# Retention attention on array quarters in 64-token steps, Strassen from the second block, and a new order of the first loads: what the change did to a kernel bound by TensorE

## The chip, the cores and the metric

The kernel runs on one core of one Trainium2 chip. The metric is device time in microseconds (us); a run is one execution on the chip, and a time quoted as "median" is the median of the runs of one kernel in one session. "Span" is the time from the first to the last instruction in the profile of one execution. The profile also gives the granted clock of TensorE, 1.000 being full speed.

Engine names: PE is TensorE (PEld its weight loads), DVE is VectorE, ACT is ScalarE, POOL is GpSimd, SP is SyncE, which here only issues DMA.

## The reference

Retention attention (8 batches, 8 heads, 576 tokens, head size 64) feeds a feed-forward layer with the activation h·cos(h):

```python
scores = q @ k.T / sqrt(64)                          # per batch and head
ret    = scores * where(i >= j, gamma[h] ** (i - j), 0)   # gamma[h] = 1 - 2**(-5-h)
x      = (ret @ v) -> [4608 tokens, 512]
h      = x @ w_in                                    # [4608, 2048], the "first product"
out    = (h * cos(h)) @ w_out                        # [4608, 512],  the "second product"
```

## The kernel before

Attention runs chunk by chunk. The decay is folded into q and v, so one chunk needs four groups of matmuls: *inter* (queries against the state that earlier chunks left), *state* (add k·v of this chunk), *intra* (masked scores against v), and *scores* of the next chunk. The tokens go through the feed-forward layer in nine blocks of 512. The second product uses one level of Strassen (7 half-size products in place of 8) from block 2 on.

A chunk here is 128 tokens of one batch, five per batch (the fifth has 64). State, intra and scores use half of the 128x128 array per matmul, and matmuls on the two halves overlap (in the trace of this kernel, from 204.74 us, those of intra start in pairs 3 ns apart, a pair of 128 columns every 56 to 59 ns):

```python
def mm_intra(self, g, box):
    ...
    for c in range(4):
        for hp in range(2):                       # two halves of the array
            inst = e.matmul(
                ap(self.BK[box.i], 512, 64 * hp, 64, c * 128, [1, n]),      # n = 128 tokens
                ap(na, 2 * DM, 0, n, DM + (2 * c + hp) * D, [1, D]),
                ap(pt, 1024, 0, n, hp * 512 + c * 128, [1, n]), ...)
```

Nothing is issued in program order. The program is a list of operations with what each reads and writes. A scheduler that runs when the kernel is built (`arrange`) plays them through with estimated costs and a simple model of the DMA rings. It fixes the order of instructions on every engine, hands out PSUM banks, and puts *filler* matmuls (on zeros) where it believes PE idle in the first 24 us. On the chip every engine then works through its fixed list and waits on semaphores: an operation placed early in the list holds up everything behind it.

The start-up:

```python
load_to(4)                                        # q, k, v of the first four chunks, on SP's queue
for g in range(4):
    self.cast_k(g, "act")
    if pair(g):
        self.cast_q(dbl(g), ("dve", "pool"))      # the two halves of the q weighting
    self.cast_v(g, "dve" if g == 3 else "pool")
    self.step_tk(g, "act")                        # transposes of k on PE, copied out by ACT
    if pair(g):
        self.step_tq(dbl(g), "dve")
    self.step_s(g); self.step_st(g); self.step_o(g)   # state and output copies on ACT
self.load_win(0, 1, [("stg", 1, 1)])              # w_in, on POOL's queue: not before v of chunk 1
self.load_win(1, 1, [("stg", 1, 1)])
self.load_win(2, 2, [("stg", 2, 1)])              # not before v of chunk 2
self.load_win(4, 2, [("stg", 2, 1)])
self.load_win(6, 2, [("stg", 2, 1)])
for x in range(4):
    self.load_wout(x, [("stg", 2, 1)])
load_to(9, [("wout", 2)])                         # block 1's q, k, v: only after w_out
... # then mlp1 (first product) of block 0
```

Block 0 is the first 512 tokens: four chunks. Their attention has to be done before "dense" work, the unbroken row of first-product matmuls, can begin. "Gates" below are the third arguments of `load_win`: what a load waits for before it is issued.

Of the kernel before, what the change touches and what calls it, by code (L numbers as in the profile page):

```python
# [14 lines left out]
CH = 128  # L15
CHUNKS = [(b, r, min(CH, S - CH * r)) for b in range(B) for r in range(5)]
TB = 512
NTB = TOK // TB
FILL, SLOW = 24.0, 5.6
NF = DFF // 128  # L20
HF, HB = NF // 2, TB // 2
XR = 3 * TB

# [9 lines left out]
class Op:  # L33
    __slots__ = ("eng", "fn", "r", "w", "sem", "cost", "ring", "deps", "need", "val", "snap",
                 "n", "out", "n_in", "start", "boxes", "seq", "port", "lazy")
# [6 lines left out]
class Prog:  # L42

    LAT = {"pe": 0.2, "act": 0.11, "dve": 0.14, "pool": 0.14, "sp": 0.0}
    WINDOW = {"pe": 24, "act": 12, "dve": 12, "pool": 6, "sp": 4}
# [8 lines left out]
    def add(self, eng, fn, r=(), w=(), sem=None, cost=0.1, ring=None, port=False, lazy=False):  # L54
        op = Op(eng, fn, list(r), list(w), sem, cost, ring)
        op.port, op.lazy = port, lazy
        self.ops.append(op)
        return op


    def arrange(self, filler, fill_until):
# [40 lines left out]
        while left:  # L102
            for eng in queue:
                while free[eng] <= now:
                    pick = None
                    for op in queue[eng][:self.WINDOW[eng]]:
                        if op not in ready or ready[op] > now:
                            continue
                        if any(b.i is None for b in op.boxes) and not banks:
                            continue  # L110
                        if op.ring and eng == "sp" and len(rings["sp"]) >= 4:
                            continue
                        if pick is None or not op.lazy:
                            pick = op
                        if not pick.lazy:
                            break
                    if pick is None:
                        if eng == "pe" and 1.4 <= now < fill_until:
                            op = Op("pe", filler, ["one", "dum"], ["fill"], None, 0.108, None)
# [3 lines left out]
                        break  # L123
                    for b in pick.boxes:
                        if b.i is None:
                            b.i = banks.pop(0)
# [23 lines left out]
            for h in heads:  # L150
                h[1] -= step / len(heads)
            for q in rings.values():
                if q and q[0][1] <= 0:
                    done.append((now + 1.25, q.pop(0)[0]))
# [65 lines left out]

def ap(t, size, p0, n, off, *dims):
# [3 lines left out]
class Kernel:  # L225
    def __init__(self, nc, es, q, k, v, w_in, w_out, out):
        self.nc = nc
        self.P = Prog(nc, es, 5)
# [3 lines left out]
        self.NSTG, self.NNAT, self.NKT, self.NQ, self.NQT = 5, 6, 5, 3, 4  # L232
# [11 lines left out]
        self.SBD = [sb(f"sbd{i}", [128, 512], BF16) for i in range(self.NSB)]  # L244
# [7 lines left out]
        self.WT = sb("wt", [128, 88], F32)  # L252
        self.IDN = sb("idn", [128, 128], BF16)
        self.TRI = sb("tri", [128, 128], BF16)
        self.ONE = sb("one", [128, 128], BF16)
        self.DUM = sb("dum", [128, 512], BF16)
        self.IV = sb("iv", [128, 88], F32)
        self.LV = sb("lv", [128, 88], F32)
        self.CLN = sb("cln", [128, 1], F32)
        self.CPI = sb("cpi", [128, 1], F32)  # L260
        self.SC = nc.alloc_psum_tensor("sc", [128, 1024], F32)
        self.ST = nc.alloc_psum_tensor("st", [128, 512], F32)
        self.BK = [nc.alloc_psum_tensor(f"bk{i}", [128, 512], F32) for i in range(5)]
        self.n_cb = self.n_os = 0

# [10 lines left out]
    def constants(self):  # L276
        P = self.P
        lng = [math.log(1.0 - 2.0 ** (-5.0 - h)) for h in range(H)]
        P.add("pool", lambda e: e.iota(ap(self.IV, 88, 0, 128, 0, [1, 40]), [[128, 5], [0, 8]], base=0,
                                       channel_multiplier=1, allow_small_or_imprecise_dtypes=True), w=["iv0"])  # L280
        P.add("pool", lambda e: e.iota(ap(self.IV, 88, 0, 128, 40, [1, 48]), [[256, 3], [1, 2], [0, 8]], base=0,
                                       channel_multiplier=2, allow_small_or_imprecise_dtypes=True), w=["iv1"])
        P.add("dve", lambda e: e.memset(self.ONE.ap(), 1.0), w=["one"])
        P.add("dve", lambda e: e.memset(self.DUM.ap(), 0.0), w=["dum"])
        for h in range(H):
            P.add("dve", lambda e, h=h: e.memset(ap(self.LV, 88, 0, 128, h, [8, 5]), -lng[h]), w=[("lv", h)], cost=0.03)
            P.add("dve", lambda e, h=h: e.memset(ap(self.LV, 88, 0, 128, 40 + h, [8, 6]), lng[h]), w=[("lv", h + 8)], cost=0.03)
        P.add("dve", lambda e: e.memset(self.CLN.ap(), math.log(1.0 / 8.0)), w=["cln"])
        P.add("dve", lambda e: e.memset(self.CPI.ap(), math.pi / 2), w=["cpi"])
        P.add("dve", lambda e: e.tensor_tensor(self.LV.ap(), self.IV.ap(), self.LV.ap(), ALU.mult),  # L290
              r=["iv0", "iv1"] + [("lv", h) for h in range(16)], w=["lvx"])
        for i in range(self.NSB):
            P.add("dve", lambda e, i=i: e.memset(self.SBD[i].ap(), 0.0), w=[("sbd", i)])
        P.add("act", lambda e: e.activation(ap(self.WT, 88, 0, 128, 0, [1, 40]), ap(self.LV, 88, 0, 128, 0, [1, 40]),
                                            AF.Exp), r=["lvx"], w=["wv"], cost=0.25)
        P.add("act", lambda e: e.activation(ap(self.WT, 88, 0, 128, 40, [1, 48]), ap(self.LV, 88, 0, 128, 40, [1, 48]),
                                            AF.Exp, bias=self.CLN.ap()), r=["lvx", "cln"], w=["wq"], cost=0.3)
# [3 lines left out]
        P.add("pool", lambda e: e.affine_select(self.TRI.ap(), self.ONE.ap(), pattern=[[1, 2], [2, 64]],  # L301
                                                compare_op=ALU.is_ge, fill=0.0, base=0,
                                                channel_multiplier=-1), r=["one"], w=["tri"])
# [7 lines left out]
    def load_kv(self, g, i, gate=()):  # L311
        b, r, n = CHUNKS[g]
        slot = g % self.NSTG
        self.P.add("sp", lambda e: e.dma_start(  # L314
            ap(self.STG[slot], 2 * DM, 0, n, i * DM, [D, H], [1, D]),
            bass.AP(self.src[1 + i], (b * H * S + CH * r) * D, [[D, n], [S * D, H], [1, D]])),
            r=list(gate), w=[("stg", slot, i)], sem=f"i{slot}_{i}", cost=0.6, ring=1.24 * n / 128)

    def load_q(self, d, gate=()):
        b, r = d // 3, d % 3  # L320
        n, slot = (128, 128, 32)[r], d % self.NQ
        self.P.add("sp", lambda e: e.dma_start(  # L322
            ap(self.QSTG[slot], 2 * DM, 0, n, 0, [2 * D, H], [1, 2 * D]),
            bass.AP(self.src[0], (b * H * S + 256 * r) * D, [[2 * D, n], [S * D, H], [1, 2 * D]])),
            r=list(gate), w=[("qstg", slot)], sem=f"q{slot}", cost=0.6, ring=1.81 * n / 128)

    def load_win(self, s, n, gate=()):
# [3 lines left out]
            r=list(gate), w=[("win", x) for x in range(s, s + n)], sem=f"wi{s}", cost=0.78, ring=1.3 * n)  # L331

    def load_wout(self, s, gate=()):
# [3 lines left out]
            r=list(gate), w=[("wout", s)], sem=f"wo{s}", cost=0.78, ring=2.6)  # L337
# [9 lines left out]
    def cast_k(self, g, eng):  # L347
        n, st, na = CHUNKS[g][2], g % self.NSTG, g % self.NNAT
        self.copy(eng, ap(self.NAT[na], 2 * DM, 0, n, 0, [1, DM]), ap(self.STG[st], 2 * DM, 0, n, 0, [1, DM]),
                  [("stg", st, 0)], [("nat", na, 0)], DM)  # L350

    def cast_v(self, g, eng):
        b, r, n = CHUNKS[g]
        st, na = g % self.NSTG, g % self.NNAT
        self.P.add(eng, lambda e: e.tensor_tensor(  # L355
            ap(self.NAT[na], 2 * DM, 0, n, DM, [D, H], [1, D]),
            ap(self.STG[st], 2 * DM, 0, n, DM, [D, H], [1, D]),
            ap(self.WT, 88, 0, n, 8 * r, [1, H], [0, D]), ALU.mult),
            r=[("stg", st, 1), "wv"], w=[("nat", na, 1)], cost=1.04 if eng == "pool" else 0.62, port=True)

    def cast_q(self, d, engs):
        n, k = (128, 128, 32)[d % 3], d % self.NQ
        for x, eng in enumerate(engs):
            self.P.add(eng, lambda e, x=x: e.tensor_tensor(  # L364
                ap(self.QNAT[k], 2 * DM, 0, n, x * DM, [D, H], [1, D]),
                ap(self.QSTG[k], 2 * DM, 0, n, x * D, [2 * D, H], [1, D]),
                ap(self.WT, 88, 0, n, 40 + 16 * (d % 3) + 8 * x, [1, H], [0, D]), ALU.mult),
                r=[("qstg", k), "wq"], w=[("qnat", k, x)], cost=1.04 if eng == "pool" else 0.62, port=True)

    def step_tk(self, g, eng="act"):  # L370
        n, k, box = CHUNKS[g][2], g % self.NNAT, Box()

        def mm(e):
            tb = self.BK[box.i].ap().bitcast(BF16)
            for c in range(4):
                inst = e.transpose(
                    tb[:, c * 128:c * 128 + n], ap(self.NAT[k], 2 * DM, 0, n, 128 * c, [1, 128]),
                    ap(self.IDN, 128, 0, n, 0, [1, n]))
            return inst

        self.P.add("pe", mm, r=[("nat", k, 0), "idn"], w=[box], cost=0.22)
        t = g % self.NKT
        dst = ap(self.KT[t], DM, 0, 128, 0, [128, 4], [1, n])

        def src():
            return self.BK[box.i].ap().bitcast(BF16)[:, 0:512].rearrange("p (c n) -> p c n", c=4)[:, :, 0:n]

        if eng == "act":
            self.P.add("act", lambda e: e.activation(dst, src(), AF.Copy), r=[box], w=[("kt", t)], cost=0.56)
        else:  # L390
            self.P.add("dve", lambda e: e.tensor_copy(dst, src()), r=[box], w=[("kt", t)], cost=0.36)

    def step_tq(self, d, eng="act"):
# [567 lines left out]
```

## Time and profile before

| | before |
|---|---|
| time, median of 3 runs | 306.48 us (306.26 to 306.99) |
| span, granted clock | 305.5 us, 1.000 |
| PE busy | 294.2 us, 96% |
| DVE / ACT / POOL busy | 76% / 58% / 51% |

The two rows below come from the page's part in which the span is cut in 40 slices, each digit a busy share in tenths; PEclk is the granted clock. The page of the kernel before:

```profile
PE   8999998999999999999999999999999999999996
...
PEclk9999999999999999999999999999999999999999
```

PE is busy everywhere, at full clock. A change pays only if it takes work or waiting from PE.

The timeline of PE of the kernel before, one attention step in mid-run (start us, us, engine, line, operation, out<-in, array tile, size, count; bracketed: idle before):

```profile
204.27 0.39 PE L473 MATMUL bk<-qt,sbd 128*128 128x128 bf16 x4
204.59 0.32 PE L458 MATMUL st<-nat 128*64 128x64 bf16 x8
204.74 0.39 PE L487 MATMUL bk<-pt,nat 128*64 128x128 bf16 x8
205.06 0.40 PE L443 MATMUL sc<-qt,kt 64*128 64x128 bf16 x8
205.39 0.28 PE L694 MATMUL bk<-wout,gt 128*128 128x256 bf16 x1
```

Read start to start, for ends are modelled: 204.27 to 205.39 is 1.12 us for 128 tokens, in inter 0.32, state 0.15, intra 0.32 and scores 0.33. Where the array tile changes (inter to state, intra to scores, scores to the dense matmul) the next start comes 149 to 152 ns after the last, where within inter, intra and scores it comes 52 to 62 ns after; this excess of about 0.1 us is the "mode change" of the prediction.

The last line of start-up on PE is the beginning of the dense work:

```profile
23.61 3.61 PE L575 MATMUL bk<-xt,win 128*128 128x256 bf16 x31
```

The chain of waits of the kernel before (start us, us, what), where the loads of block 1 come in:

```profile
19.34 16.31 DMA wout<-in_moe_w_out_dram
...
38.48 6.45 DMA qstg<-in_q_dram
...
47.10 0.62 PE bk L401 x8
```

w_out holds back a load of q, and PE's transposes (L401) wait for that q. It is the longest (1.4 us) of several pauses between 35 and 60 us, 3.2 us in all.

### The profile page before, as it was taken

What the parts mean: (1) busy time and instruction counts of PE and PEld (TensorE: products, weight loads), DVE (VectorE), ACT (ScalarE), POOL (GpSimd) and SP (SyncE); (2) the same over time, 40 slices, a digit from 0 to 9 for tenths busy, and PEclk for the clock granted to TensorE, in tenths of its full rate; (3) what the DMA queues carried; (4) which work ended last, traced back from release to release, by engine and by line L of the source; (5) the groups of instructions that cost most, each with busy time, mean ns of one, the idle gap of its engine ahead of it and who ended that gap; (6) DMA issues with size and microseconds to landing.
All of it is one profiled execution on the core that took longest, in us unless ns stands there. A gap on an engine that the chain in (4) does not pass through costs nothing.

```text
span 305.5 us, 7008 instructions
## 1 busy us (share of the span) xinstructions
PE 294.2 (96%) x2756; PEld 195.3 (64%) x2792; DVE 233.6 (76%) x349; ACT 176.1 (58%) x306; POOL 155.5 (51%) x159
## 2 busy tenths in 40 slices
PE   8999998999999999999999999999999999999996
PEld 6667434678554446766676577666765766666585
DVE  2566623789968999779899996996899669948941
ACT  5667511698466686366656656475656566546411
POOL 2870068968576664788369754854450014003213
PEclk9999999999999999999999999999999999999999
DMA  8999999999999999999999999796202100211114
GB/s 182 231 196 195 190 207 248 241 255 198 221 202 198 199 227 213 175 255 199 219 211 206 220 169 243 186 223 138 55 17 72 36 24 12 70 36 34 34 36 137
DMA packets 134432, 48.95 MB, mean 160 GB/s; under 512 B 103168, under 2 KB 133376, under 8 KB 134400
## 3 DMA queue, kind: packets, MB, share of 16 engines
q1 hardware_dynamic: 129648, 44.32, 69.3%
q0 software_dynamic: 4752, 4.19, 8.7%
q8 instruction: 22, 0.36, 0.5%
q14 instruction: 10, 0.08, 0.1%
HBM read 36.70 MB, written 9.44 MB: 151 GB/s over the span
## 4 chain that ended last, share of the span: by engine, by line
PE 75%; DMA 9%; DVE 5%; SPq 3%; issue 2%; POOL 2%; ACT 1%; DVEq 0%
PE bk L575 33%; PE bk L694 25%; PE bk L600 6%; DMA wout<-in_moe_w_out_dram 5%; PE sc L443 3%; SPq L314 3%; PE bk L487 2%; DVE gt L586 2%; DMA qstg<-in_q_dram 2%; PE st L458 2%; DMA stg<-in_v_dram 2%; PE bk L473 2%; DVE s L656 1%; SPq L322 1%; POOL win L328 1%
## 5 line engine op out<-in xcount | busy, mean ns | idle before, releaser
L575 PE MATMUL bk<-xt,win 128*128 128x512 bf16 (+3 forms) x642 | 133.3, 347 | 3.4 <-issue 0.8
L583 ACT ACTIVATE cb<-bk,cpi 128x512 bf16<-128x512 f32 (+2 forms) x152 | 100.1, 665 | 57.2 <-PE bk L575 55.0
L586 DVE TENSOR_TENSOR gt<-bk,cb 128x512 bf16<-128x512 f32 (+2 forms) x152 | 97.5, 657 | 33.8 <-ACT cb L583 32.4
L575 PEld LDWEIGHTS bk<-xt,win 128*128 128x128 bf16 x672 | 62.6, 98 | 47.3 <-ACT xt L530 1.7
L364 POOL TENSOR_TENSOR qnat<-qstg,wt 128x512 bf16<-128x512 f32 (+1 forms) x46 | 51.4, 1133 | 18.6 <-DMA qstg<-in_q_dram 18.5
L345 POOL CAST nat<-stg 128x512 bf16<-128x512 f32 (+1 forms) x36 | 24.3, 676 | 52.2 <-DMA stg<-in_k_dram 35.3
L511 DVE TENSOR_TENSOR pt<-sc,tri 128x1024 bf16<-128x1024 f32 (+1 forms) x40 | 44.3, 1107 | 8.6 <-PE sc L443 8.6
L720 POOL TENSOR_TENSOR sv<-sv,os 128x512 f32<-128x512 f32 x14 | 21.0, 1499 | 54.4 <-DVE gt L586 27.7
L355 POOL TENSOR_TENSOR nat<-stg,wt 128x512 bf16<-128x512 f32 (+1 forms) x39 | 43.6, 1117 | 2.1 <-DMA stg<-in_v_dram 1.7
L530 ACT ACTIVATE xt<-bk 128x512 bf16<-128x512 f32 (+1 forms) x41 | 27.7, 679 | 21.2 <-PE sc L443 19.8
L600 PE MATMUL bk<-wout,gt 128*128 128x512 bf16 x122 | 29.6, 379 | 0.3
L663 DVE TENSOR_TENSOR gt<-gt 128x1024 bf16<-128x1024 bf16 x28 | 28.9, 1034 | 0.0
L694 PE MATMUL bk<-tw,gt 128*128 128x256 bf16 x224 | 28.6, 273 | 0.0
L694 PE MATMUL bk<-wout,gt 128*128 128x256 bf16 x224 | 27.6, 273 | 0.9 <-DVE gt L586 0.9
L694 PE MATMUL bk<-wout,s 128*128 128x256 bf16 x224 | 27.1, 273 | 0.0
L694 PEld LDWEIGHTS bk<-wout,gt 128*128 128x128 bf16 x224 | 21.4, 98 | 7.3 <-DVE gt L586 1.8
L694 PEld LDWEIGHTS bk<-tw,gt 128*128 128x128 bf16 x224 | 21.3, 98 | 7.5 <-ACT sv L724 1.3
L656 DVE TENSOR_TENSOR s<-gt 128x1024 bf16<-128x1024 bf16 x28 | 23.5, 857 | 2.2 <-PE bk L694 2.2
L694 PEld LDWEIGHTS bk<-wout,s 128*128 128x128 bf16 x224 | 21.6, 98 | 4.9
L342 ACT ACTIVATE sbd<-st 64x256 bf16<-64x256 f32 x64 | 23.6, 370 | 1.9 <-PE st L458 0.8
L600 PEld LDWEIGHTS bk<-wout,gt 128*128 128x128 bf16 x128 | 11.8, 98 | 13.1 <-issue 0.4
L720 POOL TENSOR_TENSOR sv<-sv 128x512 f32<-128x512 f32 x7 | 9.5, 1359 | 17.9 <-ACT sv L724 17.9
(54 smaller groups left out, 239.7 us busy)
## 6 DMA issues: line engine op xcount, KB each, us to landing
out_dram<-os SPq DMA_DIRECT2D x35, 256.0 KB, 3.0
stg<-in_k_dram SPq DMA_DIRECT2D x32, 256.0 KB, 3.9
qstg<-in_q_dram SPq DMA_DIRECT2D x16, 512.0 KB, 5.3
stg<-in_v_dram SPq DMA_DIRECT2D x32, 256.0 KB, 5.3
wout<-in_moe_w_out_dram POOLq DMA_DIRECT2D x4, 512.0 KB, 15.4
win<-in_moe_w_in_dram POOLq DMA_DIRECT2D x3, 512.0 KB, 9.0
stg<-in_k_dram SPq DMA_DIRECT2D x8, 128.0 KB, 3.4
qstg<-in_q_dram SPq DMA_DIRECT2D x8, 128.0 KB, 3.4
```

Source lines behind the costliest of these rows:

```text
L355: self.P.add(eng, lambda e: e.tensor_tensor(ap(self.NAT[na], 2 * DM, 0, n, DM, [D, H], [1, D]), ap(self.STG[st], 2 * DM, 0, n, DM, [D, H], ...
L364: self.P.add(eng, lambda e, x=x: e.tensor_tensor(ap(self.QNAT[k], 2 * DM, 0, n, x * DM, [D, H], [1, D]), ap(self.QSTG[k], 2 * DM, 0, n, x ...
L511: self.P.add("dve", lambda e: e.tensor_tensor(ap(pt, 1024, 0, n, 0, [128, 8], [h, 2], [1, h]), ap(self.SC, 1024, 0, n, 0, [128, 8], [h, 2] ...
L530: self.P.add("act", lambda e, lo=lo, m=m: e.activation(ap(self.XT, 4 * XR, 0, 128, (t0 + lo) % XR, [XR, 4], [1, 2], [2, m]), ap(self.BK[bo ...
L575: inst = e.matmul(ap(self.BK[box.i], 512, 0, 128, i * n, [1, n]), ap(self.WIN, 4 * DFF, 0, 128, c * DFF + 128 * f, [1, 128]), ap(self.XT, ...
L583: self.P.add("act", lambda e: e.activation(ap(cb, TB, 0, 128, 0, [1, m]), ap(self.BK[box.i], 512, 0, 128, 0, [1, m]), AF.Sin, bias=self.CP ...
L586: self.P.add("dve", lambda e: e.tensor_tensor(ap(gt, NF * TB, 0, 128, f0 * TB + lo - TB * j, [TB, len(fs)], [1, n]), ap(self.BK[box.i], 51 ...
L600: inst = e.matmul(ap(self.BK[box.i], 512, 0, 128, 0, [1, cn]), ap(gt, NF * TB, 0, 128, f * TB + 128 * t, [1, 128]), ap(self.WOUT, NF * DM, ...
L656: self.P.add("dve", lambda e: e.tensor_tensor(ap(self.S5, HF * TB, 0, 128, f * TB, [1, 2 * TB]), ap(gt, NF * TB, 0, 128, f * TB, [1, 2 * TB]),
L663: self.P.add("dve", lambda e: e.tensor_tensor(ap(gt, NF * TB, 0, 128, f * TB + HB, [HF * TB - HB, 2], [TB, 2], [1, HB]), ap(gt, NF * TB, 0 ...
L694: inst = e.matmul(ap(self.BK[box.i], 512, 0, 128, at * HB, [1, HB]), ap(lt, lsize, 0, 128, loff + f * lstep + 128 * t, [1, 128]), ap(rt, r ...
L720: self.P.add(eng, lambda e: e.tensor_tensor(out(), a(), b(), op), r=r, w=w, cost=1.04 if eng == "pool" else 0.09 + 0.00104 * n * HB, port= ...
```

## The change

Its intent: use the array in quarters instead of halves, by working on two independent streams (batches 0, 2, 4, 6 and batches 1, 3, 5, 7) in 64-token chunks; run Strassen one block earlier; and load block 1's tokens ahead of w_out. The first 1024 tokens stay in 128-token chunks of one batch at a time, which use the array in halves as before. The core of the diff, cuts marked:

```diff
-CH = 128
+CH = 64
+EO, ES, EQ = ('dve', 'dve'), ('act', 'dve'), ('dve', 'dve')
+WI = ((0, 1, 0), (1, 1, 0), (2, 2, 0), (4, 2, 2), (6, 2, 3))
...
-        self.SC = nc.alloc_psum_tensor("sc", [128, 1024], F32)      # scores had two banks of their own
-        self.ST = nc.alloc_psum_tensor("st", [128, 512], F32)
-        self.BK = [nc.alloc_psum_tensor(f"bk{i}", [128, 512], F32) for i in range(5)]
+        self.ST = nc.alloc_psum_tensor("st", [128, 1024], F32)      # two streams' states
+        self.BK = nc.alloc_psum_tensor("bk", [128, NB * 512], F32)  # NB = 6
...
+    def mm_intra(self, g, lo):                       # x: one of two (stream, chunk) pairs
+                self.bk(lo[p0 // 64], 64 * hp, 64, c * 64, 64),
+                ap(na, 2 * DM, p0, 64, DM + (2 * c + hp) * D, [1, D]),
+                ap(pt, 1024, p0, 64, hp * 256 + c * 64, [1, 64]),
+        return [mm(c, x, hp) for c in range(4) for hp in range(2) for x in SES[g]]
...
-        load_to(4)
-        for g in range(4):
-            self.cast_k(g, "act")
-            if pair(g):
-                self.cast_q(dbl(g), ("dve", "pool"))
-            self.cast_v(g, "dve" if g == 3 else "pool")
-            self.step_tk(g, "act")
-            ...
+        load_to(need[0])
+        for g in range(need[0]):
+            cast_to(g + 1, "act", EQ, "dve" if g == 1 else "pool")   # both q halves on DVE
+            for t in tiles[g]:
+                self.step_tk(t, "dve")                               # k copies on DVE
+            for k in quads[g]:
+                self.step_tq(k, "dve")
+            self.step_s(g)
+            self.step(g, False, EO)                                  # output copies on DVE
+            self.ev_st(g, ES)                                        # states half on DVE
-        self.load_win(0, 1, [("stg", 1, 1)])
-        ...
+        for x, n, t in WI:                                           # gate: v of chunk t
+            self.load_win(x, n, [("stg", t, 1, 0)] if t >= 0 else [])
+        load_to(G1 + need[0], [("win", GT)])                         # block 1's tokens, after 2nd w_in
         for x in range(4):
-            self.load_wout(x, [("stg", 2, 1)])
-        load_to(9, [("wout", 2)])
+            self.load_wout(x, [WG])                                  # w_out after these
+        load_to(G2 + need[0], [("wout", 0)])
...
-        FIRST = 2                                                    # Strassen from block 2
+        for j in range(1, NTB): ... two = self.strassen(j, last)     # from block 1
```

Not shown: the scheduler itself was changed too. It now looks 24 instead of 12 operations ahead on ACT and DVE, and its model of the DMA rings was timed anew.

`WI` lets the first three w_in loads go once v of chunk 0 has landed (before: chunks 1, 1 and 2). `EO, ES, EQ` move start-up copies from ACT and POOL to DVE.

## The prediction

> **What bounds the kernel now.** TensorE. The page has PE busy 294.2 of 305.5 us at full clock; in the chain of waits PE holds 75%. From the timeline I divide the PE stream by what is issued (matmul start to next start): first product about 124.6 us (0.216 us per 512 columns), second 112.3, attention steps 39.5, transposes 6.1, fillers 10.4, and about 8 us in which PE waits. Of these waits about 3.2 us lie between 34.7 and 60 us (gaps of 0.48, 1.42 and 0.73 us before transposes and block 1's first product): the chain there runs w_out DMA (16.3 us, to 35.7), then q load 6.5 us, POOL scaling, transposes. The loads of block 1 were held behind w_out. The end (wait 1.1 us, then 12.1 us of Strassen) stays.
>
> **Attention on quarters.** A steady step for 128 tokens takes 1.12 us of PE before (timeline, 204.27 to 205.39): inter 4x128 columns 0.32, state 0.15, intra 0.33, scores 0.33, with three mode changes of about 0.1 each. Matmuls on the two halves of the array start 3 ns apart and each pair costs 28 ns per 64 columns. [...] If quarters behave alike, a two-stream step is: inter 8x64 columns 0.23, then state, intra and scores 4x28 ns each in one mode, two mode changes: about 0.82 us. The before total of steps (5 per batch, about 4.97 us a batch) is 39.5 us. After: 8 big chunks, scores now on their own, about 1.25 each; one lone chunk and 27 pairs, less steps with no inter: about 32.5. Saves about 7 us (estimate from these numbers).
>
> **Strassen for block 1.** 64 matmuls of 0.216 become 112 of 0.109: -1.6 us of PE; DVE gets 4 groups of token sums (1.03+0.86+0.65 us each, about 10 us) but loses about 0.5 us per mask (1.22 us for 1024 columns becomes about 0.65 for 512), about 14 us.
>
> **Added.** PE transposes go from 5 full + 2 small q and 10 + 2 k groups to 8 and 14: +1.0 us. Smaller first-product tiles: 128 more matmuls at 2.5 ns: +0.3 us. ACT copies states twice as wide (0.37 to about 0.6 us, 60 of them, +12 us) and a third table load of 1.28 us: off the critical path with ACT at 58%.
>
> **Loads.** Block 1's loads no longer wait for w_out, and w_out has two first products (27 us) to arrive. I expect 2 of the 3.2 us of waits back. w_in starts earlier beside k/v, more table preparation on DVE: start-up the same within 1 us. Steps now hold two of six PSUM banks; I allow +0.7 us of new waits.
>
> **Sum.** -7 -1.6 +1.0 +0.3 -2 +0.7 = -8.6 us, all on PE, the critical engine: **297.6 us**, 8 in 10 within **294 to 301**. Chances: faster by over 2% 0.84, within 2% 0.14, slower 0.02.
>
> **What would show it.** In the timeline a pair step takes 0.75 to 0.9 us, groups of four matmuls start a few ns apart; no PE wait over 1 us between 35 and 60 us; w_out landing before the second product of block 0; the steady PE share 97% or more; mask about 0.65 us; filler ends at about 22 us.
>
> **What would make it wrong.** Quarters not overlapping in fours (a step then 1.1 us or more, the 7 us gone); PE waiting for banks or for ACT's state and output copies, which now form a loop between successive steps; DMA, busy to 215 us (slices), falling behind through more 64-row loads and 64-row stores; start-up slowed by w_in sharing DMA with k/v; block 1's token sums on DVE holding up the second product.

## More of the kernel before

The windows of the kernel before for the start-up, busy us by engine (x instructions), then clock, DMA share and GB/s:

```profile
10.00:14.00 4.00, 4.00 (x61) 3.14 (x60) 2.75 (x3) 3.52 (x8) 3.52 (x4) 1.00 1.23 259
14.00:18.00 4.00, 3.82 (x56) 2.73 (x54) 2.68 (x3) 2.13 (x4) 3.84 (x6) 1.00 1.32 192
...
26.00:30.00 4.00, 3.95 (x30) 2.72 (x29) 3.06 (x6) 3.09 (x6) 0.00 (x0) 1.00 1.21 192
```

The columns after the length are PE, PEld, DVE, ACT, POOL. Work is spread: from 10 to 18 us DVE is busy 5.4 of 8 us, ACT 5.7, POOL 7.4.

## The result, and the profile after

| | before | after |
|---|---|---|
| time, median of 4 runs each | 306.37 us (306.19 to 306.99) | 306.02 us (305.33 to 306.82) |
| span, granted clock | 305.5 us, 1.000 | 303.4 us, 0.989 |

The ratio of the fast runs is 0.9988, 95% interval 0.9969 to 1.0007: the same. The time exceeds the span by 1.5 us before and 2.7 after in the profiled runs (1.9 and 2.3 in a later session); that small part is not explained here.

The steps themselves did what was hoped. The timeline of PE of the changed kernel, one two-stream step:

```profile
113.66 0.40 PE L529 MATMUL bk<-qt,sbd 128*128 128x64 bf16 x8
113.99 0.32 PE L550 MATMUL st<-nat 64*64 64x64 bf16 x16
114.13 0.30 PE L539 MATMUL bk<-pt,nat 64*64 64x64 bf16 x16
114.26 0.30 PE L520 MATMUL bk<-qt,kt 64*64 64x64 bf16 x16
114.50 2.79 PE L828 MATMUL bk<-wout,gt 128*128 128x256 bf16 x24
```

From 113.66 to 114.50 it is 0.84 us. In the trace the matmuls on quarters start in fours, 3 to 4 ns apart. For intra, sixteen of them take 0.13 us where eight on halves took 0.32 for the same tokens. Part of this is less work: a 64-token chunk has half as many query-key pairs per token inside the chunk. State, whose work is the same as before, takes 0.14 us (0.15 before). But the slices of the changed kernel show a hole near the left edge:

```profile
PE   8975899999999999999999999999999999999996
...
PEclk9997799999999999999999999999999999999999
```

Slices 3 to 5 (15 to 38 us) are where PE is less busy, and in slices 4 and 5 the clock is down. The windows of the changed kernel, same columns as before:

```profile
10.00:14.00 4.00, 3.95 (x43) 1.93 (x41) 3.94 (x8) 1.01 (x2) 1.25 (x2) 1.00 1.07 221
14.00:18.00 4.00, 2.84 (x38) 1.86 (x37) 3.70 (x7) 2.09 (x3) 1.80 (x2) 1.00 1.30 189
...
26.00:30.00 4.00, 1.55 (x24) 1.36 (x24) 1.02 (x2) 0.60 (x1) 4.00 (x5) 0.65 0.96 190
30.00:34.00 4.00, 3.17 (x20) 2.12 (x17) 1.34 (x3) 1.06 (x2) 0.97 (x2) 0.50 1.21 222
```

Three things are to be seen. DVE (third of the five engine columns) is full from 10 to 18 us, 7.6 of 8 us against 5.4 before, while ACT and POOL have little to do. PE stands for 2.4 us of the window from 26 to 30. From about 27 to 34 us the granted clock is one half (27.23 to 34.06 in the trace; it falls while PE still waits), and 256-column matmuls start 213 ns apart there, 109 after it. The chain of waits of the changed kernel, in the same stretch:

```profile
10.72 15.18 DMA stg<-in_v_dram
...
25.98 1.03 POOL nat L442
27.01 0.76 POOL win L416
...
27.77 0.63 POOL nat L433
...
28.45 0.61 PE bk L469 x4
...
31.10 4.98 PE bk L711 x31
```

The v load of chunk 3 takes 15.2 us: issued at 10.72 us, it lands at 25.90 (in the kernel before it was issued at 10.76 and landed at 18.96). Behind it on POOL wait its weighting, a w_in issue and the cast of the *fifth* k chunk. PE's list has the transposes of that fifth k chunk (L469), which belongs to block 1, *ahead* of the attention of chunk 3, so PE stands before them:

```profile
28.45 0.61 PE L469 MATMUL bk<-idn,nat 128*128 128x128 bf16 x4 [3.36 <-POOL nat L433]
```

The dense work begins at 31.10 us. It began at 23.61.

The whole account, obtained by sorting every matmul's time up to the start of the next one by what it computes (weight loads counted where matmul records are missing); what is left is waiting or slow clock:

| us of PE's stream | before | after | difference | predicted |
|---|---|---|---|---|
| first product | 124.1 | 124.2 | +0.1 | +0.3 |
| second product | 113.0 | 111.4 | -1.6 | -1.6 |
| attention steps | 39.5 | 32.3 | -7.2 | -7 |
| PE transposes | 6.1 | 7.7 | +1.6 | +1.0 |
| fillers, waits and slow clock up to 34.7 us | 14.1 | 21.7 | **+7.6** | within 1 |
| waits, 34.7 to 60 us | 3.2 | 1.2 | -2.0 | -2 |
| waits, 60 to 290 us | 2.2 | 2.1 | 0 | +0.7 |
| waits after 290 us | 3.3 | 2.7 | -0.6 | 0 |
| sum (the span) | 305.5 | 303.4 | -2.1 | |

So the gain was there and a new cost at the start took it. The experiments ask what that cost is made of.

### The profile page after: what moved, and what is told of

The parts are those of the page before. It is cut to its first block, busy times and chain, and to the rows that moved or that the text cites. A ratio compares the mean times of both kernels' runs of the same rounds, so it can differ in the third digit from the quotient of the medians.

```text
span 303.4 us, 8652 instructions
## 1 busy us (share of the span) xinstructions
PE 288.7 (95%) x3584; PEld 204.2 (67%) x3619; DVE 241.1 (79%) x382; ACT 189.6 (62%) x328; POOL 141.4 (47%) x138
## 4 chain that ended last, share of the span: by engine, by line
PE 83%; DMA 5%; DVE 4%; SPq 3%; issue 2%; ACT 1%; POOL 1%; DVEq 0%
PE bk L711 38%; PE bk L828 31%; DMA stg<-in_v_dram 5%; PE bk L736 5%; SPq L399 3%; PE st L550 2%; DVE gt L722 2%; PE bk L529 2%; PE bk L520 1%; PE bk L539 1%; ACT cb L719 1%; PE bk L469 1%; PE bk L481 1%; SPq L410 1%; DVE s L790 0%
## 5 line engine op out<-in xcount | busy, mean ns | idle before, releaser
L711 PE MATMUL bk<-xt,win 128*128 128x512 bf16 (+2 forms) x772 | 137.5, 320 | 5.6 <-DMA win<-in_moe_w_in_dram 1.7
L719 ACT ACTIVATE cb<-bk,cpi 128x512 bf16<-128x512 f32 x144 | 98.2, 688 | 59.9 <-PE bk L711 58.5
L722 DVE TENSOR_TENSOR gt<-bk,cb 128x512 bf16<-128x512 f32 x144 | 97.3, 686 | 36.9 <-ACT cb L719 31.9
L442 POOL TENSOR_TENSOR nat<-stg,wt 128x512 bf16<-128x512 f32 x35 | 40.5, 1158 | 27.7 <-DMA stg<-in_v_dram 27.7
L584 ACT ACTIVATE sbd<-st 64x512 bf16<-64x512 f32 (+1 forms) x68 | 39.3, 577 | 14.0 <-PE bk L520 7.8
L452 POOL TENSOR_TENSOR qnat<-qstg,wt 128x512 bf16<-128x512 f32 x30 | 36.0, 1219 | 9.3 <-DMA qstg<-in_q_dram 9.3
L433 POOL CAST nat<-stg 128x512 bf16<-128x512 f32 x32 | 25.6, 800 | 16.1 <-DMA stg<-in_k_dram 16.1
L584 ACT ACTIVATE xt<-bk 128x256 bf16<-128x256 f32 (+1 forms) x60 | 24.4, 472 | 2.7 <-DVE pt L565 2.4
L794 DVE TENSOR_TENSOR s<-gt 128x512 bf16<-128x512 bf16 x32 | 21.3, 674 | 0.0
L565 DVE TENSOR_TENSOR pt<-bk,tri 128x512 bf16<-128x512 f32 (+3 forms) x35 | 20.2, 590 | 1.1 <-PE bk L520 0.9
```

The lines of the kernel that those rows point to most:

```text
L433: self.P.add(eng, lambda e: e.tensor_copy(dst, src), r=r, w=w, cost=cost, port=eng == "pool")
L442: self.P.add(eng, lambda e: e.tensor_tensor(ap(self.NAT[na], 2 * DM, 0, 128, DM, [D, H], [1, D]), ap(self.STG[st], 2 * DM, 0, 128, DM, [D, ...
L452: self.P.add(eng, lambda e, x=x: e.tensor_tensor(ap(self.QNAT[slot], 2 * DM, 0, 128, x * DM, [D, H], [1, D]), ap(self.QSTG[slot], 2 * DM, ...
L584: self.P.add(eng, (lambda e: e.activation(*io(), AF.Copy)) if eng == "act" else (lambda e: e.tensor_copy(*io())), r=r, w=w, cost=0.127 + 0 ...
L711: inst = e.matmul(self.bk(box.i, 0, 128, i * n, n), ap(self.WIN, 4 * DFF, 0, 128, c * DFF + 128 * f, [1, 128]), ap(self.XT, 4 * XR, 0, 128 ...
L719: self.P.add("act", lambda e: e.activation(ap(cb, TB, 0, 128, 0, [1, m]), self.bk(box.i, 0, 128, 0, m), AF.Sin, bias=self.CPI.ap(), scale= ...
```

## The experiments

A yardstick for the start-up: **first-product work done by 34.7 us**, counted as us at full clock (0.109 us for 256 columns). The kernel before has done 13.75 us of it by then, the changed kernel 5.79, and in a second session 6.66. The suspects were: (a) w_in beside k and v makes k and v late; (b) PE's fixed order puts block 1's transposes ahead of block 0's attention; (c) the pause halves the clock. "Theory 1" in the texts is that (a) makes (b) wait and (b) brings (c); each text names its rivals, among them that the order alone makes the whole loss. A fourth suspect, (d) DVE overloaded from 10 to 18 us, came up only after several runs.

### Is it the changed kernel at all: run again, and matmul order within a step

`after_again` is the changed kernel unedited.

> The changed kernel unedited, as a control beside the other runs of this chip. In its first trace two of the sixteen parts of the fourth v chunk landed at 24.8 and 25.9 us, the other fourteen by 22.2; in the run with fillers, which has the same loads, all were in by 22.2. If those stragglers belong to the program, they are there again and the time is 306; if they are chance or the chip's, the time here is 302.5 to 304.5, and then most of what the added fillers and the changed order seemed to win was not theirs.

Measured: 306.44 us (305.92 to 308.91), ratio 1.0002. v of chunk 3 landed at 22.73 us without stragglers, and PE still waited, until 27.0:

```profile
27.02 0.40 PE L469 MATMUL bk<-idn,nat 128*128 128x128 bf16 x4 [2.93 <-POOL nat L433]
...
28.95 7.43 PE L711 MATMUL bk<-xt,win 128*128 128x256 bf16 x35 [0.83 <-DVE xt L584]
```

What ended the wait here was the fifth k chunk's own load, which landed at 26.30 us. So the wait does not hang on one late part of the v load; this run is the control for the start-up from here on.

`after_halves` issues a two-stream step one stream after the other:

```diff
-        return [mm(c, x, hp) for c in range(4) for hp in range(2) for x in SES[g]]
+        return [mm(c, x, hp) for x in SES[g] for c in range(4) for hp in range(2)]   # scores, intra, state alike
```

> The changed kernel with the matmuls of the two-stream steps issued one stream after the other, so that neighbours alternate between two quarters and not four; same matmuls, same results. If the quarters' overlap is what makes the steps short (0.84 us in the trace against 1.12 before) and PE bounds that part, each of 27 steps grows by three times 0.11 us, +9 us over the control. If steps are hidden behind other waits, the time moves by less than 3 us.

Measured: 307.75 us (305.8 to 309.3), ratio 1.0026. Attention rose from 31.9 to 34.5 us only. This missed its expectation by far, and the times overlap with the control's (305.9 to 308.9). It is not a clean test: state and intra still take 0.15 and 0.13 us in this order (eight pairs at the 28 ns of the kernel before would take 0.22, an estimate), so it did not undo the overlap of the quarters. It does not touch the start-up.

### Gates back, scheduler free

`gates_as_before`:

```diff
-WI = ((0, 1, 0), (1, 1, 0), (2, 2, 0), (4, 2, 2), (6, 2, 3))
+WI = ((0, 1, 1), (1, 1, 1), (2, 2, 2), (4, 2, 2), (6, 2, 2))
```

> The changed kernel with the five w_in loads held as the kernel before held them: the first two behind the second v chunk, the other three behind the third (the change lets three of them start behind the first v chunk). Theory 1 (w_in takes DMA from the start-up's k and v loads): the fourth v chunk lands at about 19 us instead of 25.9, dense first products start at 24 to 25 us instead of 31.1, no fall of the granted clock, and the time is 299 to 300.5 us. Rival A (bytes are conserved: what v gains w_in loses): dense products start but stop again for w_in, and the time stays above 304. Rival B (the order of PE, which puts the transposes of the fifth k chunk ahead of the fourth chunk's attention): the scheduler's order changes too, so this run cannot tell that by itself.

Measured: 303.79 us (302.92 to 304.21), ratio 0.990 (0.988 to 0.992), clock 1.000. v of chunk 3 lands at 19.67 us, first-product work by 34.7 us is 10.35. Better, but short of what was expected: 3.4 us of the yardstick are still missing against the kernel before, and the scheduler, given other arrival times, planned the whole program anew, with new waits later (1.5 us of PE before the group at 201.3 us). The new plan also puts the fifth k chunk's transposes at 32.5 us, behind the start of the dense work (25.56), so this run undoes (b) together with (a).

### The same fault put into the kernel before

`before_early_win` and, cleaner, `before_early_win2`, which moves only three gates of the kernel **before**:

```diff
-        self.load_win(0, 1, [("stg", 1, 1)])
-        self.load_win(1, 1, [("stg", 1, 1)])
-        self.load_win(2, 2, [("stg", 2, 1)])
+        self.load_win(0, 1, [("stg", 0, 1)])
+        self.load_win(1, 1, [("stg", 0, 1)])
+        self.load_win(2, 2, [("stg", 0, 1)])
```

(`before_early_win` also moved the fifth w_in load to v of chunk 3, where it fell behind w_out and landed at 38.45 us.)

> The mirror: the kernel before, with its w_in loads let go as early as the change lets them (three behind the first v chunk, one behind the third, one behind the fourth) and nothing else. Theory 1: the fourth v chunk lands at about 25 us instead of 18.9, the dense stretch starts 5 to 7 us later, the time is 310 to 313 us. Rival A (conserved): within 1.5 us of 306.4, for w_in is there earlier.

Measured: 318.99 us, ratio 1.0395 (1.034 to 1.045), clock 0.984; above the expected 310 to 313, and confounded by the fifth load.

> The mirror made cleaner: the kernel before with only the first three w_in loads let go behind the first v chunk; the last two and w_out keep their gates (in before_early_win the last w_in piece fell behind w_out, which added a wait of its own). Theory 1: fourth v chunk at 22 to 24 us instead of 19.0, time 309 to 312. Rival A (conserved): within 1.5 us of the kernel before.

Measured: 314.9 us (314.0 to 317.1), ratio 1.027 (1.023 to 1.032), clock 0.984, first-product work by 34.7 us 4.26 instead of 13.75. Early w_in gates cost 8 us in a kernel with nothing else of the change, more than expected (309 to 312). v of chunk 3 landed at 27.63 us, where 22 to 24 was expected. The timeline of PE says through what:

```profile
21.66 0.40 PE L376 MATMUL bk<-idn,nat 128*128 128x128 bf16 x4 [2.43 <-ACT nat L342]
...
28.40 0.43 PE L458 MATMUL st<-nat 128*64 128x64 bf16 x8 [3.55 <-DVE nat L355]
```

PE waits for chunk 3's own k (landed at 20.95 us, cast by ACT) and v (weighted by DVE), without anything of block 1 in front. A mean clock of 0.984 over the span of 312.6 us is about 10 us at one half, as are its windows from 22 to 34 us (0.60, 0.50 and 0.62). PE stood for 3.55 of them, so about 3 of the 8 us are the clock's, an estimate, and the rest is waiting. This settles that the gates can do the harm in this kernel; it does not say how much of the changed kernel's loss is theirs.

What the gates do on the DMA side can be read in the trace: from 14 to 20 us of the changed kernel, 1197 packets of the k/v queue pass beside 1202 of the w_in queue. In 2 us these are 367 to 461 k/v packets, where 1713 (6 to 8 us) and 1496 (8 to 10 us) pass on this queue before the first of w_in. A k or v packet here is 256 bytes, a w_in packet 512 or 1024 (packet records of the same trace). The k load of chunk 3 took 12.1 us from issue to landing (9.73 to 21.85), against 5.6 us in the kernel before (9.69 to 15.28). The sums of packets over the 6 us agree, but in single stretches of 2 us the ratio of k/v to w_in packets is 0.7 to 1.6; how the two queues take turns is not shown.

### Undoing only PE's order, and only the clock

`after_order` makes the fifth k chunk's transposes depend on the attention of chunk 3; on PE nothing else changes place in the start-up:

```diff
-        self.P.add("pe", mm, r=[("nat", na, 0), "idn"], w=[box], cost=0.22)
+        self.P.add("pe", mm, r=[("nat", na, 0), "idn"] + [("big", 3)] * (t == 4), w=[box], cost=0.22)
```

> The changed kernel with one extra dependency: the transposes of the fifth k chunk come after the fourth chunk's attention on PE instead of before it. Theory 1 (the wait is for v): the attention starts when v is scaled, at about 27.0 instead of 28.9 us, and the time falls by 1 to 2 us, to 304 to 305. Rival B (the order is the cause): most of the 7 us comes back, time 299 to 300.5.

Measured: 302.68 us (301.14 to 302.82), ratio 0.986 (0.983 to 0.989), clock 0.994, yardstick 8.62. Between the two expectations: the order is worth about 4 us, with half-clock time shortened as well.

`after_warm` leaves order and loads alone and puts 14 fillers (on zeros, into a bank not in use at that time) in front of these transposes:

```diff
+        at = self.ops.index(self.warm)           # the fifth k chunk's transposes
+        self.ops[at:at] = [Op("pe", self.fill2, ["one", "dum"], ["fill2"], None, 0.216, None) for _ in range(14)]
```

> The changed kernel with 14 filler matmuls (about 3 us) put into the 3.4 us in which PE waits at 24.9 to 28.3 us. The loads stay late. If the half clock granted from 27.1 to 33.9 us follows from that idle stretch and costs time by itself, the clock stays at 1.0 throughout and the time falls by 1.5 to 2.2 us, to about 304. If the lower clock costs nothing (DMA is what is waited for), the time stays at 306.

Measured: 302.41 us (302.1 to 302.73), ratio 0.986 (0.984 to 0.988). The timeline of PE:

```profile
24.14 2.97 PE L705 MATMUL st<-dum,one 128*128 128x512 bf16 x13 [0.16 <-issue]
...
28.86 5.39 PE L719 MATMUL bk<-xt,win 128*128 128x256 bf16 x39 [0.83 <-DVE xt L589]
```

Dense work begins at 28.86 us, as in the control (28.95), but 39 matmuls take 5.39 us where 35 took 7.43. The windows from 30 to 34 us, of the control and of this run:

```profile
30.00:34.00 4.00, 4.00 (x20) 2.88 (x19) 1.92 (x3) 1.37 (x2) 1.40 (x3) 0.50 0.88 194
```

```profile
30.00:34.00 4.00, 3.95 (x31) 2.90 (x30) 3.14 (x5) 3.26 (x5) 0.61 (x1) 1.00 0.76 167
```

The half clock alone is worth 4.0 us (spans 304.1 and 300.1). That is about twice what was expected. A mean clock of 0.989 over 304.1 us is 3.3 us of clock lost, that is 6.7 us at one half, an estimate (the control's windows from 26 to 38 us, at 0.76, 0.50 and 0.89, give 6.8). With matmuls at 213 ns in place of 109, as measured above, these 6.7 us lose the same 3.3 us of work; the measured 4.0 agrees within the scatter of the control's spans (303.2 to 306.2 us in four runs).

`order_warm` does both, with 6 fillers before the attention of chunk 3 and 3 before the moved transposes.

> As after_order, with 6 filler matmuls on zeros ahead of the attention of chunk 3 and 3 ahead of the fifth k chunk's transposes, so that PE is never idle for more than about 0.5 us between 22 and 28 us. after_order still had 3.4 us at half clock. Theory 1: full clock throughout, dense first products from 27.7 us as in after_order, worth half of 3.4 us: 300.5 to 301.5 us. Rival (the clock does not hang on idle time but on when the dense work starts): clock still half for some us, 302 to 303 us.

Measured: 301.29 us (301.07 to 301.4), ratio 0.9805 (0.9764 to 0.9847), span 299.2, clock 1.000, yardstick 10.35: as expected, and the lowest median of all kernels run.

`k4_behind` moves the transposes further back, behind the first dense matmuls, without added fillers (the dependency is on `"m1"`, written by block 0's first product for tokens 256 to 512).

> The changed kernel with the fifth k chunk's transposes placed behind the first 40 matmuls of the dense first product (after_order put them only behind the attention of chunk 3, and PE still stood 0.7 us before them). Nothing else of the start-up changes; the scheduler moves a few instructions between 35 and 60 us. If this wait was all that PE order cost, dense work starts near 27.4 us, limited by the attention of chunk 3, which waits for k chunk 3 (about 22 us): 301.5 to 302.7 us. If PE order costs nothing by itself (rival: only the late loads count), as after_again, 306 us.

Measured: 302.0 us (301.07 to 302.71), ratio 0.985 (0.983 to 0.987), dense from 28.03 us, clock 1.000 in the profiled run and 0.994 in two of the other three. As expected: the place of these four instructions in PE's list is worth over 4 us.

How long PE has to stand for the clock to fall is not shown by these runs. In the control the longest gap before the fall was 2.93 us. In `after_order` no gap of PE from 14 us on was over 1.4 us in the start-up and the clock was still 0.994 over 300.6 us, 3.6 us at one half (an estimate). `k4_behind`, with gaps of 1.72 and 0.82 us at the same place, kept 1.000 in its profiled run.

### Gates back in a kept order

To take the scheduler out of it, the next two add the old gates as waits after the order has been fixed, so that no instruction moves:

```diff
+        for op in self.ops:
+            op.r = op.r + op.late                # after the order is fixed
...
+            if x < 4:
+                self.P.ops[-1].late = [("stg", (1, 1, 2)[x], 1, 0)]
```

> The changed kernel with its order of instructions on every engine kept as it is, and only three extra waits: the first two w_in loads also wait for the second v chunk and the third for the third v chunk, as in the kernel before. (Giving the earlier gates to the scheduler had re-arranged the whole program; this does not.) Theory 1 (early w_in starves the k and v loads; then PE stands behind the transposes of the fifth k chunk, in order; then half clock): third v chunk and k chunk 3 land 4 to 6 us earlier, but the fifth k chunk still comes after the second w_in load, so PE still waits 2 us or more for it and the clock still drops: 304 to 306 us. Rival (the sharing alone is the loss and the order does not matter): start-up back, 299 to 301 us.

Measured: 306.96, 307.16 and 307.58 us at clock 0.989, and one run of 301.62 us at clock 1.000. PE waited 2.65 us for the fifth k chunk in the profiled run, as theory 1 had it, though three of four times lie above its 304 to 306. v of chunk 3 landed at 19.09 us instead of 22.73, and yet the dense work began no earlier: at 30.20 us (control 28.95), both runs at clock 0.989. Why the clock stayed up once was not settled.

> As the run with late gates in a kept order, and with the fifth k chunk's transposes behind the attention of chunk 3 on PE (as in the run after_order, 302.7 us). Theory 1: with both parts undone nothing is left of the start-up loss but the third table load and more transposes: dense first products from 24 to 25.5 us at full clock, no new waits later because the order is kept, so 298.5 to 300.5 us, 2.2 to 4 us below after_order and before by 6 to 8. Rival (what is left of the loss comes from the amount of data that has to come in before block 0 and not from the order of the loads): within 1 us of after_order.

Measured: 302.11 us (301.65 to 303.12), ratio 0.984 (0.979 to 0.990). v of chunk 3 landed at 18.94 us instead of 23, and next to nothing came of it against `after_order` (302.68). Theory 1 missed; its rival ("within 1 us") held. The waits on PE between 8 and 34.7 us:

```profile
PE bk L627 <- DVE pt L611: 1.4, 1, 1.4
PE bk L472 <- POOL nat L436: 1.4, 1, 1.4
PE bk L484 <- DVE qnat L455: 1.2, 1, 1.2
```

(What waits and for what; then us in total, times, longest.) Two of three are for DVE, and `after_order` had the same two (1.4 and 0.3 us). The order had been planned for late loads, and it keeps everything late: on ACT, for instance, the cast of k chunk 3 stood behind two cosines and ran at 20.3 us (in `k4_lean_late`, below) although its data had landed at 14.9.

`k4_lean_late` and `k4_lean_early` repeat the comparison with the transposes moved back as in `k4_behind` and with the 7 fillers ahead of chunk 2's attention removed; the first has the old gates added after ordering, the second has not.

> As k4_behind, with the w_in loads held back as in the kernel before (order kept, as in order_late) and without the 7 fillers (1.7 us) that stood ahead of chunk 2's attention in PE's fixed order. order_late showed that k and v chunk 3 landing 4 to 6 us earlier gains nothing as long as PE's order stays; if the order, fillers included, was what kept the gain away, then here attention of chunk 3 comes near 24.2 us and dense work near 25.5 us, at full clock: 299 to 300 us. If the loads were never the limit: as the next run, k4_lean_early.

> The same kernel as k4_lean_late except that the w_in loads go early as in the changed kernel. If early w_in costs time once PE's order no longer hides it: k chunk 3 lands near 22 us and v chunk 3 at 22 to 26 us, attention of chunk 3 at 24.5 to 27 us, and the 1.7 us of the removed fillers becomes idle time, so 1.5 to 3 us slower than k4_lean_late, with some half clock: 301 to 303 us. If early w_in does not matter: within 0.7 us of k4_lean_late.

Measured: 301.54 us (300.31 to 303.29), ratio 0.984, and 302.2 us (301.27 to 302.5), ratio 0.985; both 8.71 on the yardstick. No difference that these runs can show. Removing the fillers gained nothing either: in their place PE waited 1.5 us for DVE's mask (the masking of the scores). Expectation missed; what it says is that in this order DVE and the list limit the start, and earlier data alone did not help.

### Gates and engines, scheduler free: two by two

`gates_and_engines` is `gates_as_before` with the start-up copies back where they were, except those of k, which stay on DVE (0.42 us each); `engines_only` has the second line without the first:

```diff
-WI = ((0, 1, 0), (1, 1, 0), (2, 2, 0), (4, 2, 2), (6, 2, 3))
+WI = ((0, 1, 1), (1, 1, 1), (2, 2, 2), (4, 2, 2), (6, 2, 2))
-EO, ES, EQ = ('dve', 'dve'), ('act', 'dve'), ('dve', 'dve')
+EO, ES, EQ = ('act', 'act'), ('act', 'act'), ('dve', 'pool')
```

> The changed kernel with w_in held as the kernel before held it (as in gates_as_before, 303.8 us) and also the start-up's engines as before: copies of x and of states on ACT, q scaled on DVE and POOL. Theory: what that run still lost in the start-up (dense products from 25.6 us, the kernel before from 23.6) is the DVE's chain of scaling, two mask halves, x and state copies for one chunk after another. Then dense products start at 23.5 to 24.5 us and the time is 301 to 302.5. Rival: k and v loads of block 1 behind w_in cost it; then it stays at 303 to 304.

> The fourth cell of a two by two: w_in early (as changed) but the start-up copies of block 0's attention outputs and states on ACT and half of each q weighting on POOL, as in the kernel before, and planned again by the scheduler. In the other cells dense first products begin at 28.95 us (changed kernel, run again), 25.56 us (gates undone) and 23.6 us (gates and engines undone). DVE, which was busy for 7.6 of the 8 us from 10 to 18 us in the changed kernel, should fall to about 5.5 us there. If late k and v loads alone set the start (they land near 22 to 25 us): dense work from 27 to 29 us and PE still waits over 2 us. If DVE was the limit: dense from 25 to 26 us. The new plan has its own waits later, about as in gates_and_engines, so 304 to 308 us in the first case and 302 to 303.5 us in the second; the start of the dense work is the reading that counts.

| first-product work by 34.7 us; median time; clock | copies on DVE | copies on ACT and POOL |
|---|---|---|
| w_in early | 6.66 us; 306.44; 0.989 | 8.71 us; 306.24; 0.994 |
| w_in as before | 10.35 us; 303.79; 1.000 | 12.09 us; 303.43; 1.000 |

The gates are worth 3.7 and 3.4 us of start-up, the engines 2.1 and 1.7; the two nearly add up. (The gates' figure includes the clock, which is below 1.000 in the upper row alone.) But every cell is a new plan, and the plans differ in (b) too: the fifth k chunk's transposes stand ahead of chunk 3's attention in the first cell alone (27.02 us), and behind it in the three others (`engines_only` 26.64, `gates_as_before` 32.53, `gates_and_engines` 30.65). So 3.7 and 2.1 contain the order, and 3.4 and 1.7 do not; `after_order`, which undoes the order alone, reaches 8.62, as much as `engines_only` (8.71). The 1.7 rests on one profile each, and the times of these two kernels overlap (302.92 to 304.21 and 302.66 to 303.95).

`engines_only` began its dense work at 27.54 us, inside the first case of its expectation, but not by that case's path. k of chunk 3 landed at 16.02 us, not near 22; v of chunk 3 landed at 23.67 and was weighted by 24.78. The last wait was for DVE's mask:

```profile
25.84 0.40 PE L624 MATMUL bk<-qt,sbd 128*128 128x128 bf16 x4 [1.99 <-DVE pt L608]
```

The chain back from it runs over chunk 3's k transposes, which stood in PE's list behind first-product matmuls that waited for w_in (landed at 20.74 us). So this run does not show that late k and v set its start. Its total of 306.24 us shows no gain: waits after 60 us are 5.9 us against the control's 3.5. The windows of `gates_and_engines`:

```profile
10.00:14.00 4.00, 3.70 (x40) 1.99 (x41) 4.00 (x7) 1.98 (x4) 2.77 (x4) 1.00 1.28 248
14.00:18.00 4.00, 3.71 (x50) 2.44 (x50) 1.67 (x4) 2.70 (x5) 3.26 (x4) 1.00 1.38 214
...
26.00:30.00 4.00, 3.95 (x34) 3.11 (x32) 3.41 (x6) 3.20 (x6) 0.61 (x1) 1.00 1.20 275
```

DVE is still full to 14 us but free after that, PE no longer pauses (3.95 us of the window from 26 us, at full clock), and waits and slow clock up to 34.7 us are 4.75 us (5.37 before the change, 12.29 in the control). Yet 303.43 us missed the expected 301 to 302.5: PE waits appear later, the longest of them here:

```profile
200.53 0.72 PE L828 MATMUL bk<-wout,gt 128*128 128x256 bf16 x5 [2.29 <-DVE gt L722]
```

`gates_eng_fill` asks whose waits these are. It differs from `gates_and_engines` in one number of the scheduler, the time until which fillers are planned and one bank is held back:

```diff
-FILL, SLOW = 24.0, 5.6
+FILL, SLOW = 25.0, 5.6
```

> gates_and_engines with the time until which the scheduler plans fillers and keeps one bank back raised from 24 to 25, which makes it plan a different order further on. gates_and_engines had its start-up back but then waited, among others, 2.3 us for DVE at 198 us. If those waits belong to the order that the plan happened to take and not to the undone gates, they change here while the start-up stays (dense from about 23.6 us): 299.5 to 302 us. If they come with the later gates, as gates_and_engines within 0.7 us: 303 to 304 us.

Measured: 302.08 us (301.67 to 302.51), ratio 0.983 (0.979 to 0.987), at the upper end of the first case. The start-up stays (11.65 on the yardstick); from 180 to 202 us the waits fall from about 3 us to 0.2, and others, about 2 us, appear between 110 and 121. So these waits belong to the order that the plan happens to fall into, not to the gates. An order with both a good start and no new waits was not found.

## Why the prediction was wrong

Point by point:

- **Attention, -7 us: right.** A two-stream step takes 0.84 us (predicted 0.82), the total 32.3 us (predicted 32.5).
- **Strassen, -1.6: right. Smaller tiles, +0.3: measured +0.1. Transposes, +1.0: measured +1.6.**
- **Waits between 35 and 60 us, 2 of 3.2 back: right**, 1.2 are left. **New waits in mid-run, +0.7:** none in the first profile (2.1 us after 60 us, 2.2 before), 1.3 us more in the control's (3.5).
- **"start-up the same within 1 us": the step that failed.** It lost 7.6 us, and this is the whole difference between the predicted fall of 8.6 us and the fall of 2.1 us in the span, but for about 1 us. The same sentence names two things that could slow it ("w_in starts earlier beside k/v, more table preparation on DVE"), and the list of risks names "start-up slowed by w_in sharing DMA with k/v". No number was put on either. The table preparation did no harm: DVE's first weighting of q began at 6.57 us (6.64 before). What the prediction lacked was the path to PE: it had no wait of PE before block 1's transposes (3.36 us, 2.93 in the control), no fall of the clock after it (6.7 us at one half), and no start-up copies moved to DVE.

What the runs showed in its place:

1. Early w_in delays k and v. Shown alone in the kernel before, where three gates cost 8 us (`before_early_win2`). In the changed kernel they take 3.4 us of start-up when the plan is made anew each time (two by two, right-hand column), and nothing that the runs show when the plan is kept (point 3).
2. Start-up copies moved to DVE fill it from 10 to 18 us. With the gates as before, moving most of them back gave 1.7 us of start-up in one profile and no difference in time that these runs can show (two by two, lower row). How much of the 7.6 us is theirs stays open.
3. These reach PE through fixed lists. PE stood before block 1's transposes, with block 0's attention behind them. Moving four instructions gains 4 us with loads and engines as changed (`after_order`, `k4_behind`), and loads that come earlier gain nothing as long as the lists stay (`late_gates` against `after_again`, `order_late` against `after_order`, `k4_lean_late` against `k4_lean_early`).
4. The pause halves the granted clock for 6.7 us (an estimate from the mean of 0.989), worth 4.0 us by itself (`after_warm`, at 1.000, against `after_again`). It is part of the 7.6, not on top.

These effects overlap, so their sizes must not be summed: several remedies get back about 4 us each, and in each of these the half clock is shorter or gone. The best kernel run, `order_warm`, has 10.35 us of first product done by 34.7 us and 301.29 us in all. The 3.4 us by which it trails the kernel before on the yardstick is nearly the gap to the predicted 297.6 (3.7 us).

Open: what in the changed scheduler or the changed loads made the plan put block 1's transposes first; how the loss divides between gates and DVE; why two runs of the same program can differ in clock (`late_gates`); whether an order exists that keeps both the start-up of `gates_and_engines` and the quiet middle of the changed kernel; and 0.4 to 1.2 us by which time minus span grew.

## What to carry to other kernels

In a kernel whose engines follow fixed lists, cost the start-up of a change as carefully as its steady state: list for each early load what now passes beside it (here 367 to 461 packets of k and v in 2 us beside w_in's, 1496 to 1713 before), add up each engine's work before the first dense stretch, and check in the order of instructions whether anything that waits for a later load stands ahead of what the dense work needs. A pause of PE is paid twice when the clock falls after it, so a few fillers in front of a wait that cannot be avoided can be worth more than half of the wait (here they gained 4.0 us at a wait of 2.93). When an experiment undoes a cause in a scheduled kernel, run it both with the plan kept and with a new plan, for a plan made for late data keeps everything late.
